# A fused linear-attention and feed-forward kernel: second part in groups of 512 tokens, its first product by Strassen's scheme from the third group on

## Chip, cores and metric

One core of one Trainium2 chip. The metric is the device time of one execution in microseconds (us), the median of the runs shown. Engines: TensorE (PE) multiplies matrices, VectorE (DVE), ScalarE (ACT) and GpSimd (POOL) work element by element, SyncE (SP) issues the DMAs. TensorE writes its results to PSUM, eight banks of 128 partitions x 512 numbers of 32 bits; GpSimd works in SBUF only here.

## What is computed

The reference has two parts. Attention on 8 x 8 heads of 576 tokens and 64 features, with a feature map of 2 x 128; then a feed-forward layer on the 4608 tokens that come out of it, 512 to 2048 to 512:

```python
proj = q @ w_phi;  proj -= max|proj|          # the same for k
phi = concat(exp(proj), exp(-proj))
x = (phi(q) @ (phi(k).T @ v)) / (phi(q) @ sum(phi(k)) + 1e-6)
h = x @ w_in                                  # 4608 x 512 by 512 x 2048
g = h - tanh(h)
out = g @ w_out                               # 4608 x 2048 by 2048 x 512
```

The weights w_in and w_out come as 64-bit floats and are turned into 32-bit ones on the chip.

## The kernel before

**First part** (`period`, up to line 511). 32 units of two heads each, one unit per period of about 9.9 us, with several units in flight. Beside it each period decodes one block of weights (`dec_load`, `dec_0` to `dec_3`): 32 blocks in all, 16 row blocks f of w_in (name `wi`) and 16 of w_out (`wo`). The result of each unit goes to DRAM (`xs`).

**Second part** (from line 513). A product of 32-bit accuracy is made of fast matmuls (type fp32r) with every operand split into a high part (`wh`, `xh`, `gh`: the rounded copy) and a low part (`wl`, `xl`, `gl`: the rest): high times high, high times low, low times high, so three matmuls for each product. The 36 tiles of 128 tokens go in 12 groups g of three (384 tokens), and for each group a loop goes over the 16 blocks f. That makes 192 steps (g, f). In a step:

- `stage1` (line 525): h = w_in block times x, 4 pieces of 128 of the inner dimension x 3 parts = 12 matmuls of 384 columns into one PSUM bank (`ph`, line 533). Then g = h - tanh(h), with a polynomial where h is small: five ScalarE operations (lines 540 to 548: `y`, `s1`, `th`, `s2`, `mk`) and five VectorE ones (lines 549 to 555), of which lines 552 and 554 read the bank `ph` and the other three read SBUF alone.
- `split_g` (line 558), one step later: `gh` on ScalarE (line 561), `gl` on GpSimd (line 562).
- `stage2` (line 565), two steps later: out += g times w_out, 3 tiles x 3 parts = 9 matmuls of 512 columns into three banks `po` (lines 568, 569, 571).

The x of the next group is loaded and split during the steps of this one (`x_load`, `x_split`, lines 107 and 113), and the weight blocks that were not split during the first part (nine of each side) are split during the first group (`split_w`, line 83). All split weights stay in SBUF. The order of the second part comes from the framework's scheduler, with some instructions pinned to the order of the program (`pin`); the first part is written out by hand.

Of the kernel before, what the change touches and what calls it, by code (L numbers as in the profile page):

```python
# [27 lines left out]
def f32(ap):  # L28
    return ap.bitcast(F32)
# [3 lines left out]
def tile_linear_attention_moe(  # L33
# [22 lines left out]
    G = 3  # L56
    AHEAD = 7
# [4 lines left out]

    pin = tc.keep_in_program_order
# [10 lines left out]
    wpool = ctx.enter_context(tc.tile_pool(name="wpool", bufs=2 * NF + 2))  # L74
    tail = ctx.enter_context(tc.tile_pool(name="tail", bufs=2))
    xs = [dram.tile([NHP, P, PC], F32, name=f"xs{i}") for i in range(NBP)]

    wpa = ctx.enter_context(tc.tile_pool(name="wpa", bufs=1, reuse_waits="tile"))
    xp0 = ctx.enter_context(tc.tile_pool(name="xp0", bufs=1, reuse_waits="tile"))
    wi, wo, wp, xp = {}, {}, [], []  # L80


    def split_w(n, pin=lambda ins: ins):
        d, nm, f = (wi, wo)[n % 2], "io"[n % 2], n // 2
        early = f < AHEAD
        w = d[f]
        wh = (wpa if early else wp[0]).tile([P, DM], F32R, name=f"wh{nm}{f}")
        wl = wpool.tile([P, DM], F32R, tag="w", name=f"wl{nm}{f}")
        if early or nm == "i":
            pin(nc.scalar.copy(wh, w))  # L90
        else:
            pin(nc.vector.tensor_copy(wh, w))
        d[f] = (wh, wl)

        def low(*cut):
            cols = slice(*cut)
            pin(nc.gpsimd.tensor_tensor(wl[:, cols], w[:, cols], f32(wh[:, cols]), ALU.subtract))  # L97

        return [lambda o=o: low(o, o + DM // 2) for o in (0, DM // 2)] if early else [lambda: low(0, DM)]

    def x_tiles(g):
        pool = xp0 if g % 2 == 0 else xp[0]
        xh = pool.tile([P, NCT, G * P], F32R, tag="xh", name=f"xh{g}")
        xl = pool.tile([P, NCT, G * P], F32R, tag="xl", name=f"xl{g}")
        return xh, xl, {}

    def x_load(g, xt, c):
        bp, o = divmod(g * G, TPP)
        x = xp0.tile([P, G * P], F32, tag="x", name=f"x{g}_{c}", bufs=4)
        nc.sync.dma_start(x, xs[bp][c, :, o * P : (o + G) * P])  # L110
        xt[2][c] = x

    def x_split(xt, c, order=lambda ins: ins):
        xh, xl, x = xt
        order(nc.scalar.copy(xh[:, c, :], x[c]))
        order(nc.vector.tensor_tensor(xl[:, c, :], x[c], f32(xh[:, c, :]), ALU.subtract))  # L116

    with ExitStack() as c1:
# [232 lines left out]
        def den_recip(u, pin=lambda ins: ins):  # L355
# [4 lines left out]
            pin(nc.vector.reciprocal(rn, dn))  # L360
# [48 lines left out]
        lows = []  # L409

        def period(i):
# [28 lines left out]
            if 0 <= n < 4 * AHEAD and n % 2 == 0:  # L440
                lows.extend(split_w(n // 2))
# [5 lines left out]
            if 0 <= n < 4 * AHEAD:  # L447
                lows.pop(0)()
# [224 lines left out]
```

## Time and profile before

| | |
|---|---|
| time, median of 3 runs | 1143.04 us (1142.5 to 1143.06) |
| profiled execution | 1142.88 us |
| its span, first to last instruction | 1141.1 us |
| mean granted clock of TensorE | 0.999 |
| ScalarE busy | 829.3 us (73%) |
| GpSimd busy | 418.9 us (37%) |
| moved by DMA | 85.61 MB, mean 75 GB/s |

The profile page sums busy time by engine and by groups of instructions (line, engine, operation, tiles, shape, count, busy us, mean ns of one). "PEld" is the loading of weights into TensorE, which overlaps the matmuls. Matmuls are pipelined: the duration of one record is longer than the step from one to the next, which is what counts in a row of many. The chain of waits is followed back from the last instruction; its pieces are net times, one after the other.

### The profile page before, as it was taken

Reading aid. Unit: us, or ns where it says so; the run is one execution under the profiler, and the core shown is the slowest. Engines: PE = TensorE matmul, PEld = TensorE weight load, DVE = VectorE, ACT = ScalarE, POOL = GpSimd, SP = SyncE. Lnnn points to the kernel's source line nnn. Section 1 sums busy time; section 2 is a strip of 40 time slices with the busy share of each in tenths; the row PEclk is TensorE's granted clock in tenths of the full one; section 3 lists DMA queues with packets and bytes.
Section 4 is the critical chain, followed back from the end, with each engine's and each line's share of the span. In section 5 each row is a group of like instructions: output and inputs, shape, how many; then the busy total and the mean of one; then the engine's idle time right before and its main releaser. Section 6 shows DMA issues by size and latency. Waiting matters only on the chain.

```text
span 1141.1 us, 21052 instructions
## 1 busy us (share of the span) xinstructions
PE 1131.7 (99%) x7578; PEld 950.3 (83%) x7578; DVE 866.3 (76%) x1428; ACT 829.3 (73%) x1908; POOL 418.9 (37%) x441
## 2 busy tenths in 40 slices
PE   8999999999999999999999999999999999999998
PEld 6666666666678899999999999999999999999996
DVE  6888888888878877777767777777777777777765
ACT  5888888888887776677667677666776667676665
POOL 4665666666627722222222222222222222222222
PEclk9999999999999999999999999999999999999999
DMA  4566666666622110101001000000101000000000
GB/s 159 179 209 208 216 203 210 192 214 217 210 79 63 40 42 15 35 14 36 17 13 42 14 35 15 36 14 16 42 14 36 15 25 25 14 29 1 28 1 28
DMA packets 51176, 85.61 MB, mean 75 GB/s; under 512 B 13312, under 2 KB 28032, under 8 KB 51072
## 3 DMA queue, kind: packets, MB, share of 16 engines
q1 hardware_dynamic: 50912, 84.20, 22.8%
q8 instruction: 60, 0.98, 0.4%
q14 instruction: 44, 0.36, 0.1%
q10 hardware_dynamic: 160, 0.07, 0.0%
HBM read 65.08 MB, written 19.02 MB: 74 GB/s over the span
## 4 chain that ended last, share of the span: by engine, by line
PE 96%; DVE 2%; POOL 1%; ACT 1%; issue 1%; DVEq 0%; POOLq 0%
PE ph L533 34%; PE po L568 11%; PE po L571 11%; PE po L569 11%; PE pp L212 7%; PE pc L272 6%; PE po L317 6%; PE pd L332 3%; PE ptt L239 2%; PE pk L286 1%; PE ptr L245 1%; POOL gl L562 0%; PE warm L138 0%; DVE xl L116 0%; POOL wli L97 0%
## 5 line engine op out<-in xcount | busy, mean ns | idle before, releaser
L562 POOL TENSOR_TENSOR gl<-s,gh 128x384 fp32r<-128x384 f32 x192 | 195.3, 1017 | 575.8 <-ACT gh L561 563.2
L540 ACT ACTIVATE y<-ph 128x384 f32<-128x384 f32 x192 | 94.5, 492 | 237.6 <-PE ph L533 237.6
L533 PE MATMUL ph<-xh,wli 128*128 128x384 f32 x768 | 260.2, 339 | 0.7 <-POOL wli L97 0.7
L533 PE MATMUL ph<-xl,whi 128*128 128x384 f32 x768 | 259.7, 338 | 0.0
L533 PE MATMUL ph<-xh,whi 128*128 128x384 f32 x768 | 259.0, 337 | 0.0
L549 DVE SCALAR_TENSOR_TENSOR s<-s,y 128x384 f32<-128x384 f32 x192 | 112.3, 585 | 170.6 <-ACT s L542 170.6
L568 PE MATMUL po<-who,gh 128*128 128x512 f32 x576 | 227.0, 394 | 0.8 <-ACT gh L561 0.8
L569 PE MATMUL po<-wlo,gh 128*128 128x512 f32 x576 | 226.1, 392 | 0.0
L571 PE MATMUL po<-who,gl 128*128 128x512 f32 x576 | 164.6, 394 | 0.4 <-POOL gl L562 0.4
L533 PEld LDWEIGHTS ph<-xh,whi 128*128 128x128 f32 x768 | 145.8, 190 | 8.4 <-issue 0.5
L533 PEld LDWEIGHTS ph<-xl,whi 128*128 128x128 f32 x768 | 144.2, 188 | 8.1
L533 PEld LDWEIGHTS ph<-xh,wli 128*128 128x128 f32 x768 | 144.3, 188 | 1.1 <-POOL wli L97 1.0
L555 DVE COPY_PREDICATED s<-mk,th 128x384 f32<-128x384 uint32 x176 | 123.6, 702 | 18.5 <-DVE th L554 0.5
L571 PEld LDWEIGHTS po<-who,gl 128*128 128x128 f32 x576 | 108.0, 188 | 25.4 <-POOL gl L562 1.5
L281 POOL TENSOR_TENSOR ss<-ss,kp 128x512 f32<-128x512 f32 x96 | 123.0, 1281 | 8.1 <-ACT kp L266 3.2
L568 PEld LDWEIGHTS po<-who,gh 128*128 128x128 f32 x576 | 109.0, 189 | 19.4 <-ACT gh L561 2.0
L222 DVE TENSOR_REDUCE m<-pp 128x4 f32<-128x512 f32 (+3 forms) x98 | 92.1, 941 | 41.3 <-PE pp L212 37.8
L569 PEld LDWEIGHTS po<-wlo,gh 128*128 128x128 f32 x576 | 108.0, 187 | 16.9
L542 ACT ACTIVATE s<-y,bias_t 128x384 f32<-128x384 f32 x192 | 118.5, 617 | 2.0 <-POOL gl L562 1.9
L548 ACT ACTIVATE mk<-y,bias_t 128x384 f32<-128x384 f32 x192 | 117.8, 614 | 0.0
L266 ACT ACTIVATE kp<-t 128x256 f32<-128x256 f32 (+2 forms) x256 | 108.7, 483 | 8.2 <-DVE t L229 7.5
L551 DVE SCALAR_TENSOR_TENSOR s<-s,s 128x384 f32<-128x384 f32 x176 | 98.2, 558 | 17.6 <-ACT mk L548 0.5
(352 smaller groups left out, 1717.1 us busy)
## 6 DMA issues: line engine op xcount, KB each, us to landing
qk<-in_qkT SPq DMA_DIRECT2D x31, 576.0 KB, 6.0
v<-in_v SPq DMA_DIRECT2D x32, 320.0 KB, 4.0
rb<-rr SPq DMA_DIRECT2D x64, 144.0 KB, 3.2
xs<-rb SPq DMA_DIRECT2D x32, 288.0 KB, 2.8
x<-xs SPq DMA_DIRECT2D x48, 192.0 KB, 2.4
out<-o SPq DMA_DIRECT2D x36, 256.0 KB, 2.3
rawi<-in_moe_w_in SPq DMA_DIRECT2D x16, 512.0 KB, 4.9
rawo<-in_moe_w_out SPq DMA_DIRECT2D x16, 512.0 KB, 4.7
```

Of the source, the lines that this page charges most:

```text
L266: nc.scalar.activation(o, x, AF.Exp, scale=1.0 - 2.0 * s)
L281: nc.gpsimd.tensor_tensor(u.ss, u.ss, u.kp[:, :, j], ALU.add)
L533: nc.tensor.matmul(h, wt[:, c * P : (c + 1) * P], x[:, c, 0:N], start=(i == 0), stop=(i == 3 * NCT - 1))
L542: nc.scalar.activation(s1, y, AF.Square, bias=bias_t[:, 0:1])
L548: nc.scalar.activation(mk, y, AF.Relu, bias=bias_t[:, 2:3])
L549: nc.vector.scalar_tensor_tensor(s1, s1, PC1, y, ALU.add, ALU.mult)
L551: nc.vector.scalar_tensor_tensor(gs, s2, PC2, s1, ALU.add, ALU.mult)
L555: nc.vector.copy_predicated(gs, mk.bitcast(U32), hh)
L562: pin(nc.gpsimd.tensor_tensor(gl, gs, f32(gh), ALU.subtract))
L568: nc.tensor.matmul(po[t], a, wo[f][0], start=(f == 0), stop=False)
L569: nc.tensor.matmul(po[t], a, wo[f][1], start=False, stop=False)
L571: nc.tensor.matmul(po[t], gl[:, t * P : (t + 1) * P], wo[f][0], start=False, stop=(f == NF - 1))
```

## The change

- **Groups.** Nine groups of 512 tokens (four tiles) in place of twelve of 384. A step is now (g, j) with a pair of blocks f = 2j, 2j+1: 72 steps. Every elementwise operation is 512 wide, and a step has two sets of them (class `Set`), one for each of two banks Y and X. A set's `y` to `mk` and first two VectorE operations run in its own step, the rest of the second set in the next; the matmuls with w_out (`q`) of both sets run in the next step.
- **The first two groups** (16 steps) multiply as before (`plain`): 2 x 12 matmuls of 512 columns, then 24 with w_out, of 512 columns.
- **From the third group on** (`FOLD = 2`, 56 steps) the pair of blocks (the two blocks of 128 outputs) times the group (two halves of 256 tokens), with the inner dimension in two halves, is a 2 x 2 product of blocks and is made from seven products of half size in place of eight (`product`): each 2 pieces x 3 parts = 6 matmuls of 256 columns, 42 in a step. Five VectorE operations add the products up: K = r1 + r6 (256 wide), K + r5 and K + r7 (one operation, 512), Y += (512), X = r5 + (256), X += (256); ScalarE copies r1 to SBUF first (256).
- **Sums of the operands.** Of x: GpSimd makes four sums (`x_sum`) and the low parts (`x_lo`) of seven operands for each group, ScalarE the high parts (`x_hi`). Of the weights: during the second group VectorE makes for each pair four differences of 256 (`t_add`) and two low parts (`t_lo`), ScalarE two high parts (`t_hi`).
- **Storage.** The decoded w_in blocks and half of the w_out blocks are stored to DRAM (`wd`) during the first part; what was not split there is loaded and split during the first group (`split_load`, `split_hi`, `split_lo`, the low parts now on VectorE). The split w_out blocks live in DRAM (`wod`) and are fetched again in every group (`wo_fetch`): two loads of 512 KB in each step.
- **Order.** The whole second part is written out by hand (`manual_schedule`, `job`, `do`, `run`). Before some GpSimd operations stands a copy of one column (`mark`, tile `gate`) that waits for the second VectorE operation of a set.

```diff
+        def product(o, g, j, n):
+            h, l = weights(j, n)
+            x = xc[g][n]
+            i = 0
+            for c in range(2):
+                k = slice(c * P, (c + 1) * P)
+                m = slice(c * HN, (c + 1) * HN)
+                for w, a in ((h, 0), (h, 1), (l, 0)):
+                    nc.tensor.matmul(o, w[:, k], x[:, a, m], start=(i == 0), stop=(i == 5))
+                    i += 1
...
+        for s in range(NS + 1):
+            one, two = sets.get((s - 1, 0)), sets.get((s - 1, 1))
...
+            if fold:
...
+                r = {1: W[:, lo_], 6: W[:, hi_], 2: Y[:, lo_], 3: Y[:, hi_], 4: X[:, lo_], 5: V[:, lo_], 7: V[:, hi_]}
...
+                for n in (1, 6, 5, 7):
+                    product(r[n], g, j, n)
+                nc.scalar.copy(K[:, 0, :], r[1])
+            elif g is not None:
+                plain(Y, g, 2 * j)
...
+            run(two, "d3", "d4", "d5")
...
+            do(s, "v0")
+            do(s, "d1")
+            run(two, "gh_")
+            run(one, "gl_")
+            run(two, "gl_")
+            do(s, "p0")
+            if fold:
+                u3 = K[:, 2, :]
+                both = u3.unsqueeze(1).broadcast_to([P, 2, HN])
+                tt(u3, r[6], K[:, 0, :], ALU.add)
+                tt(K[:, 1:3, :], V.rearrange("p (a n) -> p a n", a=2), both, ALU.add)
+                for n in (3, 2):
+                    product(r[n], g, j, n)
+                q(one, 1)
+                product(X[:, lo_], g, j, 4)
+                tt(Y, Y, K[:, 0:2, :].rearrange("p a n -> p (a n)"), ALU.add)
+                tt(X[:, hi_], r[5], u3, ALU.add)
+                tt(r[4], r[4], u3, ALU.add)
+            elif g is not None:
+                plain(X, g, 2 * j + 1)
+            q(one)
+            q(two)
+            do(s, "a")
+            if g is not None:
+                new, nxt = cur
+                run(new, "y_", "s1_", "s2_", "th_", "mk_", "d1", "d2")
+                if (s, "p1") in jobs:
+                    nc.gpsimd.tensor_copy(mark, new.s1[:, 0:1])
+                do(s, "p1")
+                run(new, "d3", "d4", "d5")
+                run(nxt, "y_", "s1_", "s2_")
+                run(new, "gh_")
+                do(s, "v1")
+                run(nxt, "th_", "mk_", "d1", "d2")
```

(`one` and `two` are the two sets of the step before, `new` and `nxt` those of this one; `d1` to `d5` are the five VectorE operations of a set, and `p0`, `p1`, `d1`, `v0` in `do` are the places where the steps' jobs are put in.)

VectorE before, two steps in the middle of the second part: the tiles `s` are the polynomial's, `th` the tanh, `ph` the bank, `mk` the mask, and `x`, `xh`, `xl` the next group's tokens.

```order
L549 SCALAR_TENSOR_TENSOR s_11_8108<-s_11_8108,y_11_8106 128x384
L551 SCALAR_TENSOR_TENSOR s_11_8110<-s_11_8110,s_11_8108 128x384
L552 SCALAR_TENSOR_TENSOR s_11_8110<-s_11_8110,ph_11_8093 128x384
L554 TENSOR_TENSOR th_11_8112<-ph_11_8093,th_11_8112 128x384
L555 COPY_PREDICATED s_11_8110<-mk_11_8114,th_11_8112 128x384
L116 TENSOR_TENSOR xl_7646<-x_3_8037,xh_7645 128x384
L549 SCALAR_TENSOR_TENSOR s_12_8151<-s_12_8151,y_12_8149 128x384
```

VectorE after, a step of the fourth group: `w`, `v`, `y`, `x` are the step's four banks, `k` the sums; `_0` marks the first set, `_1` the second.

```order
L618 SCALAR_TENSOR_TENSOR s_1_7888<-s_1_7886,x_7772 128x512
L621 TENSOR_TENSOR th_1_7892<-x_7772,th_1_7892 128x512
L624 COPY_PREDICATED s_1_7888<-mk_1_7894,th_1_7892 128x512
L905 TENSOR_TENSOR k_7906<-w_7904,k_7906 128x256
L906 TENSOR_TENSOR k_7906<-v_7905,k_7906 128x512
L911 TENSOR_TENSOR y_7898<-y_7898,k_7906 128x512
L912 TENSOR_TENSOR x_7899<-v_7905,k_7906 128x256
L913 TENSOR_TENSOR x_7899<-x_7899,k_7906 128x256
L612 SCALAR_TENSOR_TENSOR s_0_7992<-s_0_7992,y_0_7990 128x512
L615 SCALAR_TENSOR_TENSOR s_0_7992<-s_0_7994,s_0_7992 128x512
L618 SCALAR_TENSOR_TENSOR s_0_7994<-s_0_7992,y_7898 128x512
L621 TENSOR_TENSOR th_0_7996<-y_7898,th_0_7996 128x512
```

What moved: between the five operations of one set and those of the next now stand the five additions, and the last three operations of the second set stand behind the step's border, ahead of the additions of the next step.

GpSimd before has in this stretch one `gl` after another and nothing between. GpSimd after, a stretch of the fifth group's steps: `gl` of both sets, `xsum` a sum for the next group, `gate` the copy that waits for VectorE, `xc` the low part of an operand.

```order
L632 TENSOR_TENSOR gl_1_9068<-s_1_9017,gh_1_9064 128x512
L771 TENSOR_TENSOR xsum_6_9070<-xsum_5_8949,xr_8680 128x512
L923 COPY gate<-s_0_9123 128x1
L783 TENSOR_TENSOR xc_5_9119<-xsum_5_8949,xc_5_9119 128x512
L632 TENSOR_TENSOR gl_0_9191<-s_0_9125,gh_0_9144 128x512
L632 TENSOR_TENSOR gl_1_9193<-s_1_9142,gh_1_9189 128x512
```

What moved: the queue of GpSimd, which held only `gl` before, now has up to two more operations of a whole 512 columns in a step, one behind the gate and one that is free to start as soon as the `gl` before it is done.

More of the change, by code (lines that the diff above doesn't have):

```diff
@@ L101, in x_tiles @@
[L101 to L116, printed above, removed]
+    late = ctx.enter_context(ExitStack())
@@ new lines, in tile_linear_attention_moe @@
+    tail = late.enter_context(tc.tile_pool(name="tail", bufs=2, side="right"))
+    xs = [dram.tile([NHP, P, S], F32, name=f"xs{b}") for b in range(B)]
+    wod = [dram.tile([P, 2, DM], F32, name=f"wod{f}") for f in range(NF)]
+    wres = ctx.enter_context(tc.tile_pool(name="wres", bufs=1, reuse_waits="tile"))
+    xp0 = ctx.enter_context(tc.tile_pool(name="xp0", bufs=1, reuse_waits="tile"))
+    xp, hl, stage = [xp0], {}, {}
+    EARLY = [("i", 0), ("o", 0), ("o", 1), ("i", 1), ("o", 2), ("o", 3), ("i", 2), ("o", 4), ("i", 3), ("o", 5), ("i", 4), ("o", 6), ("i", 5), ("o", 7)]
@@ new lines, in tile_linear_attention_moe, with wo_tile, wo_load @@
+    LATE = [(nm, f) for f in range(NF) for nm in "io" if (nm, f) not in EARLY]
+    NE = len(EARLY)
+    SEQ = [t for e, l in zip(EARLY, LATE) for t in (e, l)] + LATE[NE:]
+    NI = sum(nm == "i" for nm, _ in EARLY)
+    NO = NE - NI
+    wd = {t: dram.tile([P, DM], F32, name=f"wd{t[0]}{t[1]}") for t in SEQ if t[0] == "i" or t not in EARLY}
+    def wo_tile(f):
+        return xp0.tile([P, 2, DM], F32R, tag="wo", name=f"wo{f}", bufs=4)
+    def wo_load(f):
+        t = wo_tile(f)
+        nc.sync.dma_start(f32(t), wod[f])
+        return t
@@ L407, in q_side @@
                     q_exp(c, e, s, pts[e])
-        lows = []
+        lows, stores = [], []
         def period(i):
@@ L499, in period @@
                 dec_3(w)
+                nc.sync.dma_start(wd[w.side, w.f], w.w)
+                while stores:
+                    stores.pop(0)()
                 denom(c)
@@ L573, in store @@
-        def store(t, po, n):
-            for i in range(n):
-                o = gp.tile([P, DM], F32, tag="o", name=f"o{t + i}", bufs=3)
-                if i == 1:
-                    nc.scalar.copy(o, po[i])
-                else:
-                    nc.vector.tensor_copy(o, po[i])
-                nc.sync.dma_start(out[(t + i) * P : (t + i + 1) * P, :], o)
-        NG = NT // G
-        steps = [(g, f) for g in range(NG) for f in range(NF)]
-        late = list(range(2 * AHEAD, 2 * NF))
@@ new lines, in t_load, with t_add @@
+        def t_load(j):
+            pool, tag = (xp[0], "xc3") if j % 2 and j < NP - 1 else (tp[0], "tp")
+            t = pool.tile([P, 2, DM], F32, tag=tag, name=f"tp{j}")
+            for k in range(2):
+                stage["t", 2 * j + k] = t[:, k, :]
+                nc.sync.dma_start(t[:, k, :], wd["i", 2 * j + k])
+        def t_add(j):
+            a, b = stage["t", 2 * j], stage["t", 2 * j + 1]
+            for o, p, m in ((a[:, lo_], b[:, lo_], a[:, lo_]), (b[:, lo_], b[:, hi_], b[:, lo_]), (b[:, hi_], b[:, hi_], a[:, lo_]), (a[:, hi_], a[:, hi_], b[:, hi_])):
+                tt(o, p, m, ALU.subtract)
```

458 lines of the change are left out of this document (336 added, 122 removed).

## The prediction

> **What bounds it now.** I read the page first (busy shares, then the chain that ended last), then the chain in order of time for the second part, then the windows.
>
> ```profile
> span 1141.1 us, 21052 instructions
> PE 1131.7 (99%) x7578; PEld 950.3 (83%) x7578; DVE 866.3 (76%) x1428; ACT 829.3 (73%) x1908; POOL 418.9 (37%) x441
> PE 96%; DVE 2%; POOL 1%; ACT 1%; issue 1%; DVEq 0%; POOLq 0%
> 200.00:250.00 50.00, 50.00 (x553) 33.91 (x553) 43.82 (x61) 41.34 (x111) 30.95 (x36) 1.00 0.66 208
> 450.00:500.00 50.00, 50.00 (x253) 45.33 (x252) 35.42 (x65) 34.91 (x76) 11.91 (x12) 1.00 0.07 25
> ```
>
> TensorE is the chain in 96% of the span, in both parts, at a full clock (1.00 in both windows). So only less time in matmuls, or a new wait of TensorE, can move the end. The chain gives net times of the matmuls:
>
> ```profile
> 329.01 2.32 PE ph L533 x12
> ...
> 482.32 2.11 PE ph L533 x12
> 484.43 0.23 PE po L568
> ...
> 485.82 0.69 PE po L571 x3
> 486.51 2.11 PE ph L533 x12
> ...
> 1127.07 2.12 PE ph L533 x12
> 1129.19 0.02 issue
> 1129.21 0.49 ACT y L540
> ```
>
> A step is 486.51 - 482.32 = 4.19 us: 12 matmuls of 384 columns in 2.11 (0.1758 each) and 9 of 512 in 2.08 (0.2311 each). 192 steps are 804.5 us. They begin at 329.0, so 1141.1 - 329.0 - 804.5 = 7.6 us of the second part are something else: waits at its start and the end's tail.
>
> **First part.** TensorE's instructions are the same; the splits are as many, in another order. New are stores of 24 decoded blocks of 256 KB and eight split ones of 512 KB, 10.5 MB in some 300 us or 35 GB/s on the 208 at a DMA share of 0.66: still under 0.8, and the loads that TensorE needs are issued two periods ahead. I count nothing; it would cost if a store in SP's queue held back the loads behind it, which TensorE would feel in each of 32 periods.
>
> **The matmuls.** 128 columns more cost 0.2311 - 0.1758 = 0.0553 us, so by that line a matmul of 256 columns takes 0.1205. No row has this type at 256 columns, each with a load of 128 x 128 weights. The nearest rows:
>
> ```profile
> 205.29 1.09 PE pp L212 x16
> 207.08 0.87 PE ptt L239 x8
> 209.28 0.65 PE pp L212 x8
> L533 PEld LDWEIGHTS ph<-xh,whi 128*128 128x128 f32 x768 | 145.8, 190 | 8.4 <-issue 0.5
> 9.57 3.88 PE L138 MATMUL warm<-ident 128*128 128x256 bf16 x34
> ```
>
> The transposes load 128 x 128 weights of 32 bits for each matmul and follow each other in 0.87 / 8 = 0.109. Eight more `pp` take 0.44: 0.110 for two that run beside each other in halves of the rows, each with 128 columns of weights. The warm-up has 256 columns in bf16 at 0.114 or less. All three say that a load of such weights can be hidden in 0.11. From above, the record of a load is 0.19, but in the 384-column row one starts every 0.176, so I bound the new matmul by 0.109 and 0.1758 and take 0.1205, nearest to the three rows.
>
> The Trainium skill (TensorE: Matmul & The Clock Gate, LDWEIGHTS) puts a load of 128 columns at 128 / 1.2 GHz, an estimated 107 ns, and its section Back-to-back issue gap a matmul of 256 columns at 109 ns, so by the page load and matmul are just even, and a step from the third group on would be an estimated 10.1 us. The same gap formula gives 162 ns for 384 columns, and the trace has 176; here the page is too fast and the trace's line decides.
>
> A step of the first two groups: 48 x 0.2311 = 11.09. From the third group: 42 x 0.1205 + 24 x 0.2311 = 5.06 + 5.55 = 10.61. Together 16 x 11.09 + 56 x 10.61 = 771.6, which is 32.9 less than 804.5. (Of it 56 x 0.48 = 27 from the seven products, the rest from fewer, wider matmuls.)
>
> **Whether VectorE keeps up.** It gets five additions a step, so it has to be costed at 512 columns:
>
> ```profile
> L551 DVE SCALAR_TENSOR_TENSOR s<-s,s 128x384 f32<-128x384 f32 x176 | 98.2, 558 | 17.6 <-ACT mk L548 0.5
> L229 DVE TENSOR_TENSOR t<-pp,m 128x768 f32<-128x768 f32 x31 | 29.7, 958 | 1.1
> L229 DVE TENSOR_TENSOR t<-pp,m 128x512 f32<-128x512 f32 x34 | 23.4, 690 | 1.2
> L579 DVE COPY o<-po 128x512 f32<-128x512 f32 x24 | 16.3, 684 | 2.5 <-PE po L571 2.5
> L281 POOL TENSOR_TENSOR ss<-ss,kp 128x512 f32<-128x512 f32 x96 | 123.0, 1281 | 8.1 <-ACT kp L266 3.2
> ```
>
> 256 columns are 0.268 us, so 0.69 at 512, 0.42 at 256. Two sets of five are 10 x 0.69 + 0.1 (the masked copy is 0.05 longer than its like, below) = 7.0; the additions 2 x 0.69 + 3 x 0.42 = 2.65; the copies of results 2 x 0.68 in 8 steps, 0.17. That is 9.8 of 10.61, against 2.8 of 4.19 before.
>
> It fits if nothing is waited for, so I walk a step, from its first matmul. Products 1, 6, 5, 7 end at 2.89, 3 and 2 at 4.34, a tile with w_out at 5.73, product 4 at 6.45, the rest at 10.61. Y += starts at 4.36, X = ends at 5.47, X += must wait for product 4: 6.47 to 6.89. The first set's five end at 10.39; the second set's first two at 11.77, its last three at 13.9, K's two additions at 15.0. Y += of the next step could start at 4.36 + 10.61 = 14.97. So VectorE comes round in step, and the wait of 1.0 us for product 4 is its reserve. TensorE asks late: the first set's `gh` and `gl` are needed at 14.95 and the second's from 18.4, and they are ready at about 13.1 and 16.2. A lag of 1.5 us costs TensorE nothing.
>
> ScalarE:
>
> ```profile
> 459.35 0.49 ACT L540 ACTIVATE y<-ph 128x384 f32<-128x384 f32 x1 [1.40 <-PE ph L533]
> 461.63 0.51 ACT L561 CAST gh<-s 128x384 fp32r<-128x384 f32 x1
> L266 ACT ACTIVATE kp<-t 128x256 f32<-128x256 f32 x128 | 48.8, 449 | 1.6 <-DVE t L229 1.2
> L266 ACT ACTIVATE kp<-t 128x512 f32<-128x512 f32 x64 | 36.9, 628 | 1.1 <-DVE t L229 1.1
> ```
>
> A set is 462.14 - 459.35 = 2.79, with 6 x 0.09 more at 512: 3.3. Two sets, one copy (0.45) and 7/8 of a high part (0.6) are 7.6 of 10.61.
>
> **The port between VectorE and GpSimd.** These rows, of the first group and of a later one, show what makes the fit tight:
>
> ```profile
> 341.41 1.29 POOL L97 TENSOR_TENSOR wli<-wi,whi 128x512 fp32r<-128x512 f32 x1
> 341.45 1.67 DVE L116 TENSOR_TENSOR xl<-x,xh 128x384 fp32r<-128x384 f32 x1
> ```
>
> ```profile
> 462.26 1.02 POOL L562 TENSOR_TENSOR gl<-s,gh 128x384 fp32r<-128x384 f32 x1 [3.17 <-ACT gh L561]
> 462.49 0.55 DVE L554 TENSOR_TENSOR th<-ph,th 128x384 f32<-128x384 f32 x1
> 463.14 0.60 DVE L555 COPY_PREDICATED s<-mk,th 128x384 f32<-128x384 uint32 x1
> ```
>
> A VectorE operation on two SBUF operands that starts just behind a GpSimd one is held until it ends (1.67 us, not 0.55); one that reads PSUM is not. Now three of a set's five read SBUF alone: 2 x (0.69 + 0.69 + 0.74) = 4.2 us a step. GpSimd has two `gl` and 11 x-operations in 8 steps, each 1.28: 4.3. Together 8.6 of 10.61, possible only side by side with VectorE's PSUM work. By the walk the first set's `gl` is ready at 10.39 + 0.6 (`gh`) + 0.12 (462.26 - 462.14) = 11.11, when VectorE's second operation of the second set (from 11.08) has the port; it then runs from 11.77 to 13.05, beside two operations that read PSUM. That is won by 0.03 us. The gated operations start behind the second operation of a set and run beside the third and fourth as well. I count no loss in the steps from the third group on, 3 us for the second group (four differences and two low parts, 0.42 x 4 + 0.69 x 2 = 3.1 more on VectorE, all in SBUF: 10.1 + copies of 11.09, with up to 1.28 lost in four of the steps) and the group borders together, most of which TensorE's late demand swallows.
>
> **DMA.** Two loads of 512 KB a step:
>
> ```profile
> rawi<-in_moe_w_in SPq DMA_DIRECT2D x16, 512.0 KB, 4.9
> ```
>
> Even one after the other 9.8 us, asked for a step and 4 us ahead (15 us): hidden.
>
> **The tail.** At the end TensorE waits for two sets of 512, not for two steps of 384; by the walk the second `gl` comes at 16.2, a tile and a half of matmuls behind it: 1 us more than now.
>
> **Sum.** 1142.9 (profiled execution, 0.2 below the median) - 32.9 + 3 + 1 = **1114 us**. It reaches from 1104 to 1124 for the hiccups (0 to 10) and 0.117 to 0.124 for the matmul.
>
> **Rivals.**
> 1. *Faster matmuls.* At the transposes' 0.109 the 42 x 56 matmuls save 0.0115 each, 27 us more: 1087. For it: the rows above; against it: the 384-column row is 13 ns over the page's gap, and that must come from somewhere. The page's 109 ns gives the same 1087.
> 2. *The port.* If the first set's `gl` comes 0.03 us sooner, the second operation waits for it in every step: 9.8 + 1.28 = 11.1 in place of 10.61, 56 x 0.48 = 27 more: 1141, no gain to speak of. The Trainium skill (SBUF - State Buffer, SBUF: two separate sides) says that whoever starts first keeps the port for a whole instruction, which is what makes this all or nothing. A second lost race would make 1213.
> 3. *Slower: the weight load sets the pace.* If the load cannot shrink below the pitch of today's 384-column row, 256 columns still take 0.1758: 42 x 0.0553 x 56 = 130 more, 1244. It decides from 0.1205 + 29 / 2352 = 0.133 on. Against it are the rows at 0.109 to 0.114; for it, that all these have other types.
> 4. That the products aren't saved is excluded by the order: 42 matmuls of 128x256 stand in each step.
>
> **Numbers.** Forecast 0.55; rival 1 0.12; rival 2 0.16, half of it a little faster (0.08), 0.03 no change, 0.05 slower; rival 3 0.12; other waits that eat all of it (stores in the first part, the second group) 0.05, 0.02 of them just to no change. Under about 0.2% a measurement of this kernel can't tell from none. Faster 0.55 + 0.12 + 0.08 = 0.75, same 0.05, slower 0.05 + 0.12 + 0.03 = 0.20. The range goes from the lower edge of rival 1, 1086, to 1148, a lost port with 0.13 more per step; left out are rival 3 and the rest of the slower ones, some 0.2. The forecast's own range is 1104 to 1124.
>
> **What would show it.** Right: in the steps from the third group on, products of six follow in 0.72, steps repeat every 10.6, VectorE's only regular idle time stands before X +=, TensorE waits for nothing but the start, the second group and the tail. Wrong: weight loads back to back with TensorE's products slower than 0.133 a matmul (rival 3); VectorE records of about 1.9 in SBUF operations, and `ph`'s successors or w_out's matmuls waiting for `gl` or VectorE (rival 2); a period of the first part over 9.9.

## The result and the profile after

The changed kernel takes 1161.07 us (median of 4 runs, 1156.01 to 1161.54), the kernel before 1142.77 in the same session (4 runs, 1142.49 to 1143.06): a ratio of 1.015, 95% interval 1.0122 to 1.0178. It is slower by 1.5%, where 1114 us was forecast. Its profiled execution took 1160.98, with a span of 1159.2.

First the head of the page and, from the timeline of TensorE in a step of the third group, one pair of products (`y`, twelve matmuls of 256 columns) and the first tile with w_out (four of 512 columns):

```profile
span 1159.2 us, 22526 instructions
PE 1114.0 (96%) x8010; PEld 895.7 (77%) x8010; DVE 968.1 (84%) x1475; ACT 862.3 (74%) x1716; POOL 525.6 (45%) x506
```

```profile
594.06 1.59 PE L714 MATMUL y<-xc,hl 128*128 128x256 f32 x12
595.49 1.08 PE L656 MATMUL po<-wo,gh 128*128 128x512 f32 x4
```

The twelve take 595.49 - 594.06 = 1.43 us to the next start, 0.119 each. The term on which the gain rested (0.1205) is right, and so are the plain steps: steps 2 to 10 last 11.05 to 11.09, forecast 11.09. (The steps of the second part are counted from 0, eight to a group of 512 tokens, each from its first matmul of the first product to the next step's.) The loss lies between the matmuls, and reading the steps' starts from the trace puts it in six places, set against the forecast's own terms:

| place | forecast | measured | more |
|---|---|---|---|
| first part, until the second starts | 329.0 | 337.3 | 8.3 |
| step 1 | 11.1 | 16.7 | 5.6 |
| steps 11 to 15 (second group, weight sums) | 55.4 | 61.1 | 5.7 |
| steps 16 to 19 (the rest of the sums) | 42.4 | 49.4 | 7.0 |
| first steps of the six later groups (12.9 to 14.4 each) | 63.7 | 79.2 | 15.5 |
| the other 46 fold steps (mostly 10.8) | 488.1 | 495.6 | 7.5 |

That is 49.6; 4 of it had been allowed for the second group, the borders and the tail, and 1.4 are left over for the rest of the second part: 47 in all. Four views of the trace after show what stands there.

**The first part.** The windows of the first part (length, then busy time of TensorE, its weight loads, VectorE, ScalarE and GpSimd, clock, DMA share, GB/s) and a row of the waits of SyncE's queue:

```profile
120.00:180.00 60.00, 58.01 (x634) 39.41 (x638) 51.41 (x71) 48.36 (x127) 34.78 (x42) 1.00 0.72 235
240.00:300.00 60.00, 56.68 (x621) 37.83 (x613) 48.75 (x69) 47.44 (x124) 33.97 (x39) 1.00 0.72 238
```

```profile
SPq L395 <- DMA rr<-rn: 101.1, 30, 5.3
```

TensorE, without a gap there before, now misses 2.0 and 3.3 us of a window of 60. The transfers rise from some 210 to some 235 GB/s. The row of waits gives the total, the number and the longest: the queue waits 30 times, 101.1 us in all and up to 5.3, for `rr`, a store of 4.5 KB on which the reciprocal of the denominators goes out to DRAM and back; in the kernel before it was 16.2 us in all and up to 2.2.

**The start of the second part.** Three rows of the timeline:

```profile
345.35 0.41 ACT L374 ACTIVATE dd<-pd 128x288 f32<-128x288 f32 x1 [4.36 <-DMA dn<-dd]
346.41 0.69 DVE L612 SCALAR_TENSOR_TENSOR s<-s,y 128x512 f32<-128x512 f32 x1 [6.81 <-ACT s L597]
350.94 0.73 PE L656 MATMUL po<-wo,gh 128*128 128x512 f32 x2 [2.42 <-ACT gh L628]
```

`dd` is one tile. The last copy into it waits 4.36 us for the transfer that reads the tile's former content, ScalarE works in order, so `s` of step 0 comes late, VectorE stands 6.81 us, `gh` is late, and TensorE waits.

**An ordinary fold step.** VectorE's rows in the timeline, from one `y +=` (L911) to the next; the round begins in the last step of the third group and ends in the first of the fourth:

```profile
609.57 0.70 DVE L911 TENSOR_TENSOR y<-y,k 128x512 f32<-128x512 f32 x1
610.17 0.42 DVE L912 TENSOR_TENSOR x<-v,k 128x256 f32<-128x256 f32 x1
610.63 0.43 DVE L913 TENSOR_TENSOR x<-x,k 128x256 f32<-128x256 f32 x1
611.75 0.69 DVE L612 SCALAR_TENSOR_TENSOR s<-s,y 128x512 f32<-128x512 f32 x1 [0.69 <-ACT s L597]
612.55 0.69 DVE L615 SCALAR_TENSOR_TENSOR s<-s,s 128x512 f32<-128x512 f32 x1
613.37 0.69 DVE L618 SCALAR_TENSOR_TENSOR s<-s,y 128x512 f32<-128x512 f32 x1
613.98 0.69 DVE L621 TENSOR_TENSOR th<-y,th 128x512 f32<-128x512 f32 x1
614.76 0.78 DVE L624 COPY_PREDICATED s<-mk,th 128x512 f32<-128x512 uint32 x1
615.43 0.68 DVE L612 SCALAR_TENSOR_TENSOR s<-s,y 128x512 f32<-128x512 f32 x1
616.22 0.69 DVE L615 SCALAR_TENSOR_TENSOR s<-s,s 128x512 f32<-128x512 f32 x1
617.01 0.69 DVE L618 SCALAR_TENSOR_TENSOR s<-s,x 128x512 f32<-128x512 f32 x1
617.61 0.69 DVE L621 TENSOR_TENSOR th<-x,th 128x512 f32<-128x512 f32 x1
618.40 0.73 DVE L624 COPY_PREDICATED s<-mk,th 128x512 f32<-128x512 uint32 x1
619.02 0.41 DVE L905 TENSOR_TENSOR k<-w,k 128x256 f32<-128x256 f32 x1
619.54 0.69 DVE L906 TENSOR_TENSOR k<-v,k 128x512 f32<-128x512 f32 x1
620.33 0.70 DVE L911 TENSOR_TENSOR y<-y,k 128x512 f32<-128x512 f32 x1
```

One round is 10.76 us (most others inside a group are 10.75 to 10.84), more than the 10.57 that a step takes where TensorE alone sets it. VectorE's only idle time in it is 0.69 us, before L612: from `y +=` ScalarE must square twice (L593, L597) before L612 has its operand. The rest is not idle, but look at the starts: L621, which needs nothing of L618, starts 0.61 us after it; L624, which needs L621's result, 0.78 after it; L612 to L615 and L615 to L618, each needing the one before, 0.80 and 0.82. The records overlap when the next instruction is independent. A row's duration of 0.69 is neither of the two spacings.

**The first step of a group.** GpSimd and TensorE in the timeline:

```profile
617.04 0.18 POOL L894 COPY gate<-s 128x1 f32<-128x1 f32 x1 [2.24 <-DVE s L615]
617.17 1.29 POOL L783 TENSOR_TENSOR xc<-xr,xc 128x512 fp32r<-128x512 f32 x1
618.42 3.06 POOL L632 TENSOR_TENSOR gl<-s,gh 128x512 fp32r<-128x512 f32 x2
620.28 0.73 PE L659 MATMUL po<-wo,gl 128*128 128x512 f32 x2 [2.11 <-POOL gl L632]
```

GpSimd stands at a gate that waits for VectorE, then makes the low part of x for product 4, and only then `gl`; TensorE waits 2.11 us for it. It looks like a cause of its own. The first experiment shows that it is not.

### The profile page after: what moved, and what is told of

Read it like the earlier page. It is cut to its first block, busy times and chain, and to the rows that moved or that the text cites. A ratio compares the mean times of both kernels' runs of the same rounds, so it can differ in the third digit from the quotient of the medians.

```text
span 1159.2 us, 22526 instructions
## 1 busy us (share of the span) xinstructions
PE 1114.0 (96%) x8010; PEld 895.7 (77%) x8010; DVE 968.1 (84%) x1475; ACT 862.3 (74%) x1716; POOL 525.6 (45%) x506
## 5 line engine op out<-in xcount | busy, mean ns | idle before, releaser
L632 POOL TENSOR_TENSOR gl<-s,gh 128x512 fp32r<-128x512 f32 x144 | 216.0, 1502 | 358.9 <-ACT gh L628 217.7
L656 PE MATMUL po<-wo,gh 128*128 128x512 f32 x1152 | 328.3, 398 | 6.9 <-ACT gh L628 5.8
L656 PEld LDWEIGHTS po<-wo,gh 128*128 128x128 f32 x1152 | 210.3, 190 | 50.1 <-ACT gh L628 6.8
L659 PE MATMUL po<-wo,gl 128*128 128x512 f32 x576 | 198.8, 408 | 20.3 <-POOL gl L632 20.2
L659 PEld LDWEIGHTS po<-wo,gl 128*128 128x128 f32 x576 | 105.5, 189 | 64.0 <-POOL gl L632 42.3
L612 DVE SCALAR_TENSOR_TENSOR s<-s,y 128x512 f32<-128x512 f32 x144 | 99.6, 692 | 52.7 <-ACT s L597 52.7
L624 DVE COPY_PREDICATED s<-mk,th 128x512 f32<-128x512 uint32 x144 | 110.1, 765 | 14.9
L597 ACT ACTIVATE s<-y,bias_t 128x512 f32<-128x512 f32 x144 | 104.3, 724 | 19.1 <-DVE s L618 9.7
L615 DVE SCALAR_TENSOR_TENSOR s<-s,s 128x512 f32<-128x512 f32 x144 | 103.6, 719 | 16.0 <-ACT gh L628 1.4
L239 PEld LDWEIGHTS pp<-wph,qk 64*128 64x128 f32 x1152 | 72.1, 187 | 40.3 <-PE po L344 13.1
L609 ACT ACTIVATE mk<-y,bias_t 128x512 f32<-128x512 f32 x144 | 102.6, 713 | 0.0
L601 ACT ACTIVATE s<-y,bias_t 128x512 f32<-128x512 f32 x144 | 102.1, 709 | 0.0
L593 ACT ACTIVATE y<-y 128x512 f32<-128x512 f32 x72 | 43.0, 598 | 66.4 <-DVE y L911 63.2
```

The lines of the kernel that those rows point to most:

```text
L239: nc.tensor.matmul(heads[e][:, o * F : (o + 1) * F], u.qk[hs, j * P : (j + 1) * P], wph[hs, :], start=True, stop=True)
L597: nc.scalar.activation(self.s1, self.y, AF.Square, bias=bias_t[:, 0:1])
L601: nc.scalar.activation(self.gs, self.y, AF.Square, bias=bias_t[:, 1:2])
L609: nc.scalar.activation(self.mk, self.y, AF.Relu, bias=bias_t[:, 2:3])
L615: stt(self.s1, self.gs, PC2, self.s1, ALU.add, ALU.mult)
L624: nc.vector.copy_predicated(self.gs, self.mk.bitcast(U32), self.th)
```

## The experiments

Theory A: every place has a cause of its own, and is cured alone (2.1 us for each border). Theory B: from step 11 on VectorE's round is the bound, 10.76 in a fold step and about 88 in a group of eight; TensorE's waits are where it shows. Of each run the table gives steps read as above; "border" is the first step of the six later groups, "next" the step behind it, "ordinary" the others of those groups (without single steps that last longer once).

| run | second part starts | step 1 | steps 11 to 15 | 17, 18 | border | next | ordinary | us (range) | ratio to before, 95% |
|---|---|---|---|---|---|---|---|---|---|
| after | 337.3 | 16.7 | 61.1 | 12.5, 13.5 | 12.9 to 14.4 | 10.5 to 10.6 | 10.5 to 10.8 | 1161.1 (1156.0 to 1161.5) | 1.0122 to 1.0178 |
| e1_border | 335.7 | 17.5 | 60.9 | 12.5, 13.5 | 11.9 | 11.8 to 13.7 | 10.8, the third 11.4 | 1166.1 (1162.9 to 1169.7) | 1.0177 to 1.0230 |
| e2_dd2 | 336.4 | 11.3 | 60.1 | 12.9, 13.5 | 12.3 to 14.5 | 10.5 to 10.6 | 10.5 to 10.8 | 1156.8 (1155.2 to 1159.2) | 1.0104 to 1.0142 |
| e3_actstore | 337.4 | 14.1 | 60.3 | 13.1, 11.9 | 12.4 to 14.5 | 10.5 to 11.3 | 10.6 to 11.4 | 1158.0 (1155.7 to 1164.6) | 1.0101 to 1.0180 |
| e4_plain | 333.7 | 17.2 | 55.2 | 11.1, 11.1 | 11.1 | 11.1 | 11.05 to 11.1 | 1147.0 (1137.8 to 1151.9) | 1.0002 to 1.0048 |
| e5_vorder | 334.5 | 13.7 | 63.8 | 13.1, 14.7 | 13.5 to 15.0 | 10.6 to 14.9 | 10.6 to 11.7 | 1181.7 (1177.0 to 1183.5) | 1.0309 to 1.0359 |
| e6_best | 332.8 | 11.7 | 66.0 | 13.1, 14.7 | 11.8 to 11.9 | 12.5 to 13.4 | 10.6 to 11.8 | 1177.1 (1172.6 to 1183.1) | 1.0267 to 1.0339 |
| e7_nowd | 328.9 | 15.4 | 59.3 | 12.5, 13.5 | 13.0 to 14.5 | 10.5 to 11.3 | 10.6 to 11.4 | 1148.8 (1147.7 to 1152.8) | 1.0038 to 1.0079 |
| e8_pbest | 333.3 | 11.7 | 55.2 | 11.1, 11.1 | 11.1 | 11.1 | 11.05 to 11.1 | 1136.7 (1132.3 to 1142.1) | 0.9934 to 0.9972 |
| e9_vtwo | 335.2 | 17.7 | 58.5 | 13.5, 14.0 | 11.2 to 12.7 | 10.8 to 15.9 | 10.57 | 1144.5 (1141.5 to 1152.3) | 0.9991 to 1.0062 |
| e10_xv | 329.2 | 12.8 | 59.4 | 13.5, 14.0 | 11.2 to 12.0 | 13.2 to 13.5 | 10.57 | 1150.8 (1144.0 to 1152.2) | 1.0033 to 1.0086 |
| e11_pbest2 | 335.5 | 11.2 | 55.2 | 11.1, 11.1 | 11.1 | 11.1 | 11.05 to 11.1 | 1134.8 (1133.8 to 1138.3) | 0.9922 to 0.9951 |
| e12_hold | 332.0 | 13.1 | 59.1 | 12.5, 13.5 | 11.2 to 12.0 | 11.8, one 13.9 | 10.57 | 1139.3 (1134.4 to 1140.2) | 0.9949 to 0.9976 |
| e13_noadd | 331.7 | 11.9 | 55.2 | 10.6, 10.6 | 10.6 to 11.8 | 11.8 to 13.2 | 10.57 | 1129.8 (1122.6 to 1134.3) | 0.9862 to 0.9918 |

### e1_border: product 4's low part before the border

```
-                (8, "p", x_lo, 4),
+                (7, "p1", x_lo, 4),
```

> The fourth sum's low part is taken in the step before the group border, right behind the second's, instead of in the border step ahead of gl. Theory A (each loss has a place of its own): the six border steps fall from 12.95 us to the 10.8 of the other steps, and the steps behind a border rise from 10.57 to 10.8, since VectorE's loop of 10.8 sets them; a group of eight goes from 88.0 to 86.4, six groups give 9.6, so 1151.5 us, and PE's wait at L659 for gl loses its 20 us. Theory B (VectorE and GpSimd are full, and what is taken away here comes back): the low part, now at the end of the step before, slows VectorE there, the borders stay over 12 us, and the time is within 3 us of 1161.

1166.1, 5 us slower. The border fell to 11.9 and TensorE's wait for `gl` with it, but the next two steps grew to 11.8 and 11.4. The timeline, GpSimd and VectorE one step before the border:

```profile
612.50 2.55 POOL L783 TENSOR_TENSOR xc<-xr,xc 128x512 fp32r<-128x512 f32 x2
612.97 0.68 DVE L621 TENSOR_TENSOR th<-y,th 128x512 f32<-128x512 f32 x1
613.75 1.93 DVE L624 COPY_PREDICATED s<-mk,th 128x512 f32<-128x512 uint32 x1
```

The masked copy takes 1.93 us instead of 0.78, since the second low part has begun beside it; L621, which reads PSUM, is not touched. VectorE loses 1.15 us, and four of the six groups are longer by 1.1 to 1.4 (the other two by 0 and 2.7). So A falls here: the wait of 2.1 us had been hidden beside VectorE's lag, and what VectorE lost counted in full. B's mechanism holds, though it had the borders at over 12 us and the time within 3 us of 1161; it was 5.

### e2_dd2: two tiles for dd

```
-            u.dd = tail.tile([P, CH], F32, tag="dd", name=f"dd{u.i}", bufs=1)
+            u.dd = tail.tile([P, CH], F32, tag="dd", name=f"dd{u.i}", bufs=2)
```

> The tile dd gets two buffers instead of one. Theory A: ScalarE no longer stands for 4.36 us at 345.35 until the load of dn has left SP's queue, step 1 falls from 16.66 us to 11.1, and the time from 1161 to 1155.5. Theory B (SP's queue is the cause, not the buffer): the next instruction in the same chain waits instead, step 1 stays over 14 us, and less than 2 us are gained.

1156.8, and step 1 is 11.3: A is right for this place. The run shows one thing more. Four of its borders last 14.4 to 14.5 us, not 12.9, with much the same wait (2.05 to 2.11 us). The windows behind one of these waits (704.47 is its end):

```profile
697.00:704.00 7.00, 5.38 (x41) 4.84 (x39) 6.35 (x11) 5.18 (x10) 4.20 (x5) 1.00 0.44 155
...
705.00:706.00 1.00, 1.00 (x7) 0.96 (x6) 0.22 (x1) 0.60 (x1) 0.65 (x1) 0.59 0.62 208
706.00:707.00 1.00, 1.00 (x4) 0.84 (x4) 0.55 (x2) 1.00 (x2) 0.00 (x0) 0.50 0.03 8
707.00:708.00 1.00, 1.00 (x4) 0.77 (x3) 0.91 (x2) 1.00 (x3) 0.00 (x0) 0.50 0.00 0
708.00:709.00 1.00, 1.00 (x5) 0.81 (x4) 0.85 (x2) 0.97 (x2) 0.00 (x0) 0.70 0.00 0
```

The granted clock is 0.5 for some 3 us behind a wait of 2.1, and the step is longer by 1.5. Behind three of the four the seven next steps run at 10.57, TensorE's own pace, as VectorE has caught up, and the group (88.3 to 88.5) is hardly longer than one of the kernel after without it (mostly 87.9 to 88.3); behind the fourth the steps go back to 10.8 after three, and the group takes 89.6.

### e3_actstore: the first part's stores from ScalarE's queue

```
-        nc.sync.dma_start(wod[f], f32(t))
+        (nc.scalar if f < NO else nc.sync).dma_start(wod[f], f32(t))
...
-                    stores.append(lambda w=w: nc.sync.dma_start(wd[w.side, w.f], w.w))
+                    stores.append(lambda w=w: nc.scalar.dma_start(wd[w.side, w.f], w.w))
```

> The weight stores of the first part are issued from ScalarE's queue instead of SP's; the bytes are the same. Theory A (SP works in order and a store that waits holds the loads behind it): the periods go back to 9.9 us and the second part starts at 330 instead of 337.3, so about 1154. Theory B (the transfers themselves are slowed by 10.5 MB more): the load chain of the denominators stays as slow, the second part starts between 335 and 340, and the time stays within 3 us of 1161; issuing on ScalarE could also cost up to 3 us.

1158.0 and a start at 337.4: B. The place of the weight stores in SyncE's queue is not what slows the first part.

### e7_nowd: 6 MB of the first part's stores left out

```
-                    stores.append(lambda w=w: nc.sync.dma_start(wd[w.side, w.f], w.w))
+                    pass
...
-            nc.sync.dma_start(w, wd[nm, f])
+            nc.sync.dma_start(w, qkT[f][:, 0:DM])
```

> Left out: the first part's 24 stores of single weight blocks of 256 KB (6 of the 10.5 MB that the change adds there); the loads that read them take the same bytes from an input. If the added bytes slow the first part (the stores issued from ScalarE's queue had left it at 337.4), the second part starts at about 333 instead of 337.3 and the time is 1156; if the 4 MB that stay are enough to slow it, or the loss has another cause, it starts between 335 and 338 and the time stays within 3 us of 1161.

The later loads of these blocks read as many bytes of an input in their place, so what is computed is not the reference's. The time is 1148.8, and the second part starts at 328.9, as in the kernel before: more than expected (1156 and 333). One window of e3_actstore and the same of this run:

```profile
240.00:300.00 60.00, 55.56 (x616) 37.61 (x614) 48.49 (x68) 47.09 (x124) 34.25 (x39) 1.00 0.76 251
```

```profile
240.00:300.00 60.00, 60.00 (x663) 40.68 (x661) 52.68 (x74) 49.87 (x131) 36.64 (x43) 1.00 0.73 237
```

The four times (1147.7 to 1152.8) all lie below the four of after (1156.0 to 1161.5), so the stored bytes are the likely cause. They are not shown to be: the rate itself does not tell the windows apart (after has 238 GB/s at a share of 0.72 with 3.3 us of gaps, e7 237 at 0.73 with none), and ten other profiles with all of the stores in SyncE's queue have the second part start anywhere between 329.2 (e10_xv) and 336.4. What goes with the loss is the wait for `rr`: 30.1 us in all in e7 and 53.4 in e10_xv, without a loss, 68 to 82 for starts of 331.7 to 337.4, 91 to 109 for 332.8 to 337.3. The times spread too: ten runs of e4_plain over 14 us, where the kernel before has less than 3. Each profile is one execution; in them the first part loses 0 to 8 us.

### e4_plain: no Strassen

```
-        FOLD = 2
+        FOLD = NG
...
-            job(s - 1, "d1", t_load, j)
-            job(s, "d1", t_add, j)
-            job(s, "a1", t_hi, j)
-            job(s + 1, "v0", t_lo, j)
```

> All nine groups go by the plain product: Strassen's seven products, its weight sums and its sums of x are left out, and the groups of 512 tokens, the storage and the first part stay. By the plain steps of the kernel after (11.06 us in steps 2 to 10): steps 11 to 15 take 55.3 instead of 61.1, and steps 16 to 71 take 619.4 where they now take 624, so 1150.5 us: Strassen as built costs some 10 us, and the rest of the loss against 1142.8 is in the first part and at the start of the second. Rival (the seven products themselves bring nothing, or the wide groups are at fault): the plain steps of the later groups are 10.8 or less, 1135 or under, or over 11.3 with stalls of their own, 1165 or more.

1147.0 (1150.5 expected, with a first part 3.6 us shorter than that of after in the profile): Strassen's products as built cost 14 us by the medians. Every step from 2 on is 11.05 to 11.1, with 8 x 11.07 = 88.6 a group against 88.0 with the seven products. So the products do save, and VectorE's round and the sums take it back.

### e5_vorder: VectorE's instructions in another order

```
-            run(two, "d3", "d4", "d5")
+            run(two, "d4", "d3")
+            if fold:
+                u3 = K[:, 2, :]
+                tt(u3, r[6], K[:, 0, :], ALU.add)
+            run(two, "d5")
...
-                    nc.gpsimd.tensor_copy(mark, new.s1[:, 0:1])
+                    nc.gpsimd.tensor_copy(mark, new.y[:, 0:1])
...
-                run(new, "d3", "d4", "d5")
+                run(new, "d4", "d3", "d5")
```

> VectorE does the same instructions in another order: in both sets the subtraction of tanh comes ahead of the product with h (so that an instruction does not follow the one whose result it needs), the first K addition of a fold step is put ahead of the second set's masked copy, and GpSimd's gate in the step reads y instead of s, so that x_lo is over before the masked copy. Theory B (VectorE's row of dependent instructions is the bound from step 11 on, 10.78 us a fold step, 88.0 a group): an instruction behind its producer starts 0.80 us after it, behind another 0.60, so the loop falls by 0.2 for each set and 0.3 for the K addition to 10.1, PE's own 10.57 becomes the pace of all ordinary fold steps, a group falls to between 85 and 86.5 us, steps 11 to 19 lose 0.4 each, and the time is between 1139 and 1150. Theory A (PE waits for gl in GpSimd's queue, each at its place): steps of 10.8 and borders of 12.95 stay, within 3 us of 1161.

1181.7: neither. The last group's steps, where GpSimd has nothing to do for a next group, are 10.59 (10.59 to 10.83 in after), as B says; the steps with a low part of x are 11.7. Two pairs of rows of the timeline and one of the waits:

```profile
622.22 1.26 POOL L632 TENSOR_TENSOR gl<-s,gh 128x512 fp32r<-128x512 f32 x1
622.36 1.73 DVE L624 COPY_PREDICATED s<-mk,th 128x512 f32<-128x512 uint32 x1
...
639.11 1.29 POOL L783 TENSOR_TENSOR xc<-xr,xc 128x512 fp32r<-128x512 f32 x1
639.69 1.25 DVE L612 SCALAR_TENSOR_TENSOR s<-s,y 128x512 f32<-128x512 f32 x1 [0.68 <-ACT s L597]
```

```profile
ACT s L597 <- DVE s L618: 81.1, 72, 2.3
```

The earlier gate puts the low part beside L612, whose operands are both in SBUF, where the gate of the changed kernel puts it beside L618 and L621, which read PSUM. And L618, now later in the first set, is the last reader of the one tile `s` that ScalarE needs for the second set: 72 waits. The edit was too wide to test B.

### e6_best: the same with e1's and e2's edits

> The order of the run before, with two buffers for dd and the fourth sum's low part taken in the step before the border. Theory B: with VectorE below PE's pace the move of the low part now helps where it cost 5 us alone, since its second collision with the masked copy is gone: borders of 11 to 12 us, groups of 84.6 to 86, step 1 at 11.1, in all 6 to 12 us under the run before: 1130 to 1143. Theory A expects 10 us for the borders and 6 for dd from 1161: 1145.

1177.1, neither case: step 1 is 11.7 and the borders 11.9, but the steps of 11.7 are there as in e5. Nothing new.

### e9_vtwo: the order of the second set alone

```
-            run(two, "d3", "d4", "d5")
+            run(two, "d4", "d3")
+            if fold and j:
+                tt(K[:, 2, :], r[6], K[:, 0, :], ALU.add)
+            run(two, "d5")
...
-                tt(u3, r[6], K[:, 0, :], ALU.add)
+                if j == 0:
+                    tt(u3, r[6], K[:, 0, :], ALU.add)
```

> Only the second set's VectorE work is put in another order (the subtraction of tanh ahead of the product with h, the first K addition ahead of the masked copy except in a group's first step); the first set and GpSimd's gates stand as in the kernel after, so that x_lo again runs beside the two instructions that read PSUM. Theory B, mended (VectorE's loop is the bound, and an instruction with both operands in SBUF stands still while GpSimd works): the loop falls from 10.78 by 0.2 and 0.3 to about 10.3, the ordinary fold steps go at PE's 10.6, none at 11.7, a group at 85 to 86.5 us, and the time is 1143 to 1151. Rival (the order was the fault in the last two runs, whatever GpSimd did): steps of 11.7 remain and the time is over 1165.

1144.5, 16.6 us less than after, without an instruction less. VectorE's rows of the second set in a fold step:

```profile
646.44 0.69 DVE L615 SCALAR_TENSOR_TENSOR s<-s,s 128x512 f32<-128x512 f32 x1
647.05 0.68 DVE L621 TENSOR_TENSOR th<-x,th 128x512 f32<-128x512 f32 x1
647.65 0.68 DVE L618 SCALAR_TENSOR_TENSOR s<-s,x 128x512 f32<-128x512 f32 x1
648.25 0.41 DVE L894 TENSOR_TENSOR k<-w,k 128x256 f32<-128x256 f32 x1
648.58 0.76 DVE L624 COPY_PREDICATED s<-mk,th 128x512 f32<-128x512 uint32 x1
649.22 0.69 DVE L910 TENSOR_TENSOR k<-v,k 128x512 f32<-128x512 f32 x1
650.01 0.70 DVE L915 TENSOR_TENSOR y<-y,k 128x512 f32<-128x512 f32 x1
```

From L615 to `y +=` are 3.57 us; in the kernel after (616.22 to 620.33) they were 4.11. The starts lie 0.6 and 0.33 apart where nothing is waited for. All ordinary steps are at 10.57, TensorE's pace. In the last group, where GpSimd makes nothing for a next one, a round of VectorE from `y +=` to `y +=` lasts 10.20 us here and 10.81 in after: the order alone takes it from above TensorE's pace to below it. B stands, in the mended form: VectorE's round is the bound, and an instruction with both operands in SBUF stands still while GpSimd works. (By steps the two profiles differ by 14.3 us, of which 2.1 lie in the first part, which the edit does not touch.)

### e10_xv and e12_hold: the border

e10 is e9 with two tiles for `dd` and with product 4's low part on VectorE; e12 adds that ScalarE copies r1 into K ahead of the group's last output tile:

```
-                (8, "p", x_lo, 4),
+                (7, "v1", x_lo, 4, nc.vector),
```

```
                 nc.scalar.copy(K[:, 0, :], r[1])
+                while ends:
+                    finish(*ends.pop(0))
...
-            while ends:
+            while ends and (not fold or j or ends[0][1] < 3):
                 finish(*ends.pop(0))
```

> The order of the run before, two buffers for dd, and the fourth sum's low part by VectorE in the step ahead of the border instead of by GpSimd in the border step. Theory B: step 1 at 11.1 to 11.7 (5.5 us less), borders of 11 to 12 without the wait of 2.1 us for gl and without the half clock behind it, groups of 85 to 86: 1134 to 1143, about level with the kernel before. Rival (VectorE is the bound still): its 0.7 us more a group are lost and the borders stay: 1143 or more.

> As the run with x_lo on VectorE (1150.8), with ScalarE's copy of r1 into K taken ahead of its copy of a group's last output tile, which waits 1.9 us for a store of 256 KB to free one of the three o tiles. Theory B: the K copy no longer stands behind that store, VectorE's first K addition no longer waits 1.33 us for it, the second step of a group falls from 13.2 to 11.5 us or less, a group to 85 to 86.5, in all 10 to 13 us: 1136 to 1142. Rival (the second step is long since the border only moved one step on, whatever ScalarE waits for): it stays over 12.5, and the time over 1146.

e10: 1150.8, where the rival had it, but not for the rival's reason: the borders did fall, to 11.2 to 12.0, and the step behind them rose to 13.2, so that the two together are no better than e9's. Its timeline, ScalarE and VectorE in that step:

```profile
619.18 0.59 ACT L667 COPY o<-po 128x512 f32<-128x512 f32 x1 [1.89 <-DMA out<-o]
619.67 0.38 ACT L887 COPY k<-w 128x256 f32<-128x256 f32 x1
620.08 0.42 DVE L894 TENSOR_TENSOR k<-w,k 128x256 f32<-128x256 f32 x1 [1.33 <-ACT k L887]
```

The fourth output tile waits for one of three buffers, that is for the store of 256 KB in front, K's copy stands behind it in ScalarE's order, and VectorE behind that. In e12 the same place reads:

```profile
618.88 0.38 ACT L887 COPY k<-w 128x256 f32<-128x256 f32 x1
620.38 0.41 DVE L896 TENSOR_TENSOR k<-w,k 128x256 f32<-128x256 f32 x1
620.80 0.59 ACT L667 COPY o<-po 128x512 f32<-128x512 f32 x1 [1.53 <-DVE k L896]
```

The wait of VectorE is gone, the step falls to 11.8, and the time to 1139.3: faster than the kernel before (0.9962, 0.9949 to 0.9976), with all of the computation in it.

### e13_noadd: without the weight sums

```
-            job(s, "d1", t_add, j)
```

> The kernel of the run before without the 32 subtractions that make the weight sums (their four instructions a step on VectorE in steps 9 to 17 are left out, the products then go by unsummed weights). If steps 11 to 18 are long because VectorE is full there, steps 11 to 15 fall from 11.9 to 11.1 us and steps 17 and 18 from 13.5 and 14 to 11 to 12: 7 to 9 us less than the run before. If the loads of these steps or GpSimd's sums of x are the cause, less than 2 us are gained.

1129.8, 9.5 us less than e12 beside it: steps 11 to 15 at 55.2, steps 17 and 18 at 10.6. The four subtractions a step on VectorE make steps 11 to 18 long. They are 4 x 0.42 = 1.7 us by their kind, but in seven of the eight steps the trace of after has 2.76 to 3.89 from the first one's start to the last one's end: both operands lie in SBUF, and the first or the last, often the first two, take 1.40 to 1.52 beside GpSimd's `gl` and its sums of x. So those sums have a share in it, through VectorE.

### e8_pbest and e11_pbest2: the plain kernel mended

Both are e4 with e2's edit and with four tiles for `o`; e11 leaves out the six stores that only the weight sums read:

```
-            o = gp.tile([P, DM], F32, tag="o", name=f"o{g}_{t}", bufs=3)
+            o = gp.tile([P, DM], F32, tag="o", name=f"o{g}_{t}", bufs=4)
```

```
-                if (w.side, w.f) in wd:
+                if (w.side, w.f) in LATE:
```

> All groups by the plain product as in the run that had 1147, with two buffers for dd and four for o. Strassen's products and sums are left out. Step 1 falls from 17.2 to 11.1 us, the waits for o cost nothing in plain steps: 1141. If the first part's spread (1138 to 1152 in ten runs) has its cause in the start of the second part, the spread shrinks too; if it lies in the first part, it stays.

> The plain kernel with two buffers for dd and four for o, and without the first part's six stores of early w_in blocks, which nobody reads when there are no weight sums (1.5 of 10.5 MB); Strassen's products and sums are left out. If the bytes slow the first part in proportion, the second part starts 1 to 2 us sooner and the time is 1134 to 1136; if not, 1137.

1136.7 (1141 expected) and 1134.8: both faster than the kernel before, with nothing of the reference left out. In e8 step 1 fell to 11.7 and the spread stayed (1132.3 to 1142.1); as every later step is level, it most likely lies in the first part. e11 is 2 us lower, but its profile starts at 335.5, so that these bytes alone are the reason is not shown.

## Why the prediction was wrong

**Right.** The matmul of 256 columns (0.119 measured, 0.1205 forecast), the plain step (11.07), the hidden loads with w_out, TensorE's share of a fold step: once VectorE is out of the way it lasts 10.57 (forecast 10.61). Rivals 1 and 3 (a matmul of 0.109 or 0.1758) are out.

**The step that failed: "VectorE comes round in step, and the wait of 1.0 us for product 4 is its reserve."** The walk set a round's 12 instructions of 512 columns at their duration, 0.69. In the trace they start 0.60 to 0.67 after one that they don't need and 0.78 to 0.82 after one that they do, and in the order as written eight of a round's fifteen need the one just before. From L612 to `y +=` a round has 8.58 us where the walk had 15.0 - 6.9 = 8.1. And the reserve before `X +=` was none: ScalarE's two squares between `y +=` and L612 fill the same time, 2.18 us from start to start, and in steady state that chain, not product 4, ends last. 2.18 + 8.58 = 10.76: 0.15 over the step of 10.61, so VectorE and not TensorE sets the groups' length. e9 shows it by order alone. The Trainium skill (VectorE: DVE Perf Modes, The DRAIN you can't avoid) says that the next operation does not start until the one before has left the pipe, though one that is not held starts earlier, and that in its row of eight copies a semaphore after each cost nothing more. The 0.60 here, under a record of 0.69, fits the earlier start; but a wait for the operation just before costs some 0.2 us here, and the measurement decides.

**"3 us" for the second group and the borders together** were 28 (5.7 + 7.0 + 15.5). With VectorE as the bound, everything that it does once a group or once in all is paid in full: two output copies (1.28), the wait for K's copy behind a store (0.5 in after, 1.33 in e10), the weight sums (9.5 by e13). The forecast set these against a slack of 10.61 - 9.8 that did not exist.

**"I count nothing" for the first part** was up to 8.3. The added stores do not do it by their place in the queue (e3). What the queue stands for is the landing of the small store `rr`, 101.1 us in all in place of 16.2, and 30.1 without 6 MB of the stores (e7). In after this came at a DMA share (0.72) still under the 0.8 named. Why this wait grows, and by so much more in one execution than in another, stays open.

**The wait for `dd`** was not in the working at all: 5.6 us, shown by e2. It depends on a tile with one buffer whose reader is a DMA behind others.

**The rival "port"** had a true mechanism in the wrong place. In the kernel after VectorE stands still for it eleven times among the subtractions of the weight sums (1.40 to 1.52 us in place of 0.42) and hardly ever in a fold step. Whether it does depends on which of VectorE's instructions stands beside GpSimd's: e1 and e5 brought the loss into the fold steps. Two of the six places, the first part and the second group, had been given a chance of 0.05 together, as "other waits".

What the seven products bring in the end can be read from e12 and e11: steps 16 to the start of the last take 603.5 against 608.8 us. 5 of the 27 us are left there; the sums in steps 11 to 15 (59.1 against 55.2) and the tail behind the last step's start (24.0 against 20.6) take these back too, and e11, without Strassen, is the fastest complete kernel here. Why the first part's loss varies from run to run, and why a border's next step is still 11.8 in e12, was not settled.

## What to carry to other kernels

When a change moves an engine from two thirds of a step to over 90%, cost its round by start-to-start distances along its own order, dependent ones apart from independent ones, and include the other engine's link in it; busy time alone says that it fits. A reserve counts only if nothing else falls due in the same gap. Before a wait of TensorE is mended, see whether the engine behind it has time to give: a wait that hides beside another engine's lag is worth nothing, and moving its cause can cost.

## What the runs showed of the hardware

- A wait of TensorE of only 2.1 us can be followed by half its clock for some 3 us (granted clock 0.5, the step 1.5 us longer), and much the same wait can leave it at 1.00: the clock fell at one of six borders in after (the wait there was 2.23 us, at the others 2.07 to 2.17) and at four of six in e2 (2.05 to 2.11). The Trainium skill (TensorE: Matmul & The Clock Gate, Why this matters for your kernels) warns of gaps over about 3 us; here less was enough.
- VectorE's start-to-start time at 512 columns is 0.60 to 0.67 us behind an independent instruction and 0.78 to 0.82 behind the one that it needs, with records of 0.69 to 0.78; the port's rule of the prediction held beside it, with the masked copy at 1.93 instead of 0.78 us where GpSimd had begun just before.
- Another order of three VectorE instructions in a step, with the same work, moved the kernel's median by 16.6 us one way (e9), and a slightly wider one by 20.7 the other way (e5).
